# Wider source elements in the contiguous loads of a two-branch attention kernel

## The chip, the cores and the metric

The kernel runs on one core of a Trainium2 chip. The metric is the device time in microseconds (us). Runs of the kernel before spread by about 1%. Every comparison below was made on one chip in alternating rounds. Words used throughout: PE is the matrix engine, DVE the vector engine, ACT the scalar engine, POOL the general engine, and SP the engine whose instruction stream starts all loads here. The core has 16 DMA engines (the page gives the queues' share of 16). The tiles in the core's memory (SBUF) span 128 partitions here.

A load ("DMA") has a source access pattern and a destination access pattern. A *source element* here is one contiguous run of the source pattern, for example 8 KB. A *piece* is one contiguous run of the destination, inside one partition. The trace records *packets*, and we will see that a packet is one source element.

## The reference

Two attention branches share one output. Branch A has 32 query heads over 4 key/value heads, branch B has 32 of each. Both have 16 batches of 32 queries, 1024 cached keys and head size 128.

```python
q = (x @ wq).reshape(B, Sq, H, Dh).transpose(0, 2, 1, 3)
scores = einsum("bhqd,bhkd->bhqk", q, k_cache) * Dh ** -0.5
o = einsum("bhqk,bhkd->bhqd", softmax(scores), v_cache)
out = o.transpose(0, 2, 1, 3).reshape(B, Sq, H * Dh) @ wo
# result: concatenate([A's out, B's out], axis=-1); all bfloat16
```

B's K and V caches alone are 134 MB each, so of the 342 MB that the kernel moves almost four fifths are B's K and V.

## The kernel before

SP issues all loads in one order that a list scheduler fixed beforehand. A load waits on SP until its buffer is free, and everything behind it in SP's stream waits too: in the profile before SP waits 347 us in all, 101 us of it at B's K loads for DVE's transposes, which free K's buffers. B's K has two buffers of 1 MB, B's V three of 1 MB (four loads of 256 KB each), A's K two and A's V one of 256 KB.

```python
def folded_load(e, dst, src):                       # source and destination patterns given as they are
    inst = mybir.InstDMACopy(..., engine=mybir.EngineType.SP, queue="qSPDynamicHW",
        ins=e.lower_ap_dma(src), outs=e.lower_ap_dma(dst))
    return e.add_instruction(inst)
...
KB_sb = sb("KB_sb", [P, NKB, 2, 16 * Dh], BF)       # P = 128 partitions, 8 KB each per buffer
VB_sb = sb("VB_sb", [P, NVB, 4, NCH, Dh], BF)       # 2 KB per partition and head
...
# B's K: 128 source elements of 8 KB -> 128 partitions of 8 KB
ksrc = pb["k"][q.b, q.h0:q.h0 + 4].rearrange("a (p s) d -> (a p) (s d)", s=32)
... e.dma_start(KB_sb[:, sl, :, :].rearrange("p i n -> p (i n)"), ksrc)
# B's V, one head: 32 source elements of 8 KB -> 128 partitions of 2 KB
vsrc = pb["v"][q.b, q.h0 + t_].rearrange("(g p c) d -> g (p c d)", p=4, c=NCH)
... folded_load(e, VB_sb[:, sl, t_, :, :].rearrange("p c d -> p (c d)"), vsrc)
# A's K and V, output weights, x: 128 source elements of 2 KB -> 128 partitions of 2 KB
... e.dma_start(KA_sb[:, sl, :, :], pa["k"][q.b, q.s].rearrange("(p c) d -> p c d", c=NCH))
... e.dma_start(woB_sb[:, h_, :], wo[r0:r0 + Dh, :])
```

So V was already "folded": one source element covers four neighbouring partitions. The q weights (wq) have strided 2 KB rows and stay as they are.

## Time and profile before

| | before |
|---|---|
| time, median of 4 runs | 850.96 us |
| DMA rate over the span | 402 GB/s |
| PE, DVE, ACT busy | 85%, 64%, 53% |
| data packets of 2 KB / 8 KB | 34560 / 32768 |

First the page of the kernel before: the slices (40 equal parts of the span; a digit is the busy share in tenths), the DMA summary with the traffic of the chip's main memory (HBM), and the chain that ended last, followed back from the last instruction to whatever released each step.

```profile
PE   3999999799988799789988788987999867877777
...
DMA  9999999999999999999999999999999999999995
GB/s 346 384 389 404 410 397 398 414 403 391 411 414 417 417 409 415 414 382 403 419 414 415 412 417 418 409 411 417 419 420 415 407 417 419 408 390 410 418 413 195
DMA packets 82075, 341.59 MB, mean 402 GB/s; under 512 B 14112, under 2 KB 14624, under 8 KB 49184
...
HBM read 337.64 MB, written 2.10 MB: 400 GB/s over the span
...
DMA 48%; PE 28%; DVE 12%; SPq 6%; issue 3%; ACT 2%; POOL 0%; POOLq 0%; DVEq 0%
DMA KB_sb<-in_B_k_cache_dram 28%; DVE KBt_sb L844 9%; DMA VB_sb<-in_B_v_cache_dram 8%; PE ps_pj L674 7%; DMA woB_sb<-in_B_wo_dram 6%; PE ps_s L879 5%; DMA VA_sb<-in_A_v_cache_dram 4%; SPq L498 4%; PE ps_pj L731 4%; PE ps_o L971 3%; PE ps_kt L937 2%; PE ps_pt L921 2%; PE ps_s L862 2%; DMA KA_sb<-in_A_k_cache_dram 1%; DMA acc<-in_B_x_dram 1%
```

The DMA engines are busy all the time, at 400 to 420 GB/s in most slices, and nearly half of the chain is DMA, the largest part of it waiting for B's K. The kernel is bound by its loads, with PE not far behind.

Then the longest waits of consumers for B's loads (who waited for what; us in total, times, longest), and the issue of loads on SP (duration of the instruction in ns as min/median/max, then first and last start).

```profile
DVE KBt_sb L844 <- DMA KB_sb<-in_B_k_cache_dram: 62.6, 67, 3.3
...
PE ps_o L971 <- DMA VB_sb<-in_B_v_cache_dram: 29.5, 27, 3.3
```

```profile
L809 SPq DMA_DIRECT2D KB_sb<-in_B_k_cache_dram x128: 327/334/1511, 14.9 to 822.9; - x128
...
DMA to landing us min/median/max: 5.1/8.6/13.5
```

A load lands 8.6 us after its issue, so some 3.5 MB are on the way at any time (an estimate: 8.6 us at 402 GB/s).

The trace also records each packet's start, duration and size. The two numbers to take from these records are the duration and the *step*, which is the time from one packet's start to the next one's on the same engine. The records do not name the engine, so the step was read as the peak in the distribution of start differences.

| packet (before) | median duration, ns | mean duration, ns | step, ns |
|---|---|---|---|
| 2 KB | 84 | 85.5 | 80 |
| 8 KB | 309 | 317.3 | 306 |
| semaphore write (4 bytes) | 9 | 9.0 | 6 |

The counts fit only if a packet is a *source* element. V's 8 KB sources, which are written as four 2 KB pieces, show as 16384 packets of 8 KB.

### The profile page before, as it was taken

Reading aid. Unit: us, or ns where it says so; the run is one execution under the profiler, and the core shown is the slowest. Engines: PE = TensorE matmul, PEld = TensorE weight load, DVE = VectorE, ACT = ScalarE, POOL = GpSimd, SP = SyncE. Lnnn points to the kernel's source line nnn. Section 1 sums busy time; section 2 is a strip of 40 time slices with the busy share of each in tenths; the row PEclk is TensorE's granted clock in tenths of the full one; section 3 lists DMA queues with packets and bytes.
Section 4 is the critical chain, followed back from the end, with each engine's and each line's share of the span. In section 5 each row is a group of like instructions: output and inputs, shape, how many; then the busy total and the mean of one; then the engine's idle time right before and its main releaser. Section 6 shows DMA issues by size and latency. Waiting matters only on the chain.

```text
span 849.6 us, 27817 instructions
## 1 busy us (share of the span) xinstructions
PE 722.7 (85%) x12104; PEld 430.9 (51%) x12104; DVE 544.4 (64%) x1117; ACT 448.5 (53%) x981; POOL 68.2 (8%) x76
## 2 busy tenths in 40 slices
PE   3999999799988799789988788987999867877777
PEld 2556655456545455445654445553655544544443
DVE  0655676467755677457785566775677756757854
ACT  1455666366644466445655445754565635555453
POOL 0000000000000000000000000000000000000000
PEclk9999999999999999989999999999999989999999
DMA  9999999999999999999999999999999999999995
GB/s 346 384 389 404 410 397 398 414 403 391 411 414 417 417 409 415 414 382 403 419 414 415 412 417 418 409 411 417 419 420 415 407 417 419 408 390 410 418 413 195
DMA packets 82075, 341.59 MB, mean 402 GB/s; under 512 B 14112, under 2 KB 14624, under 8 KB 49184
## 3 DMA queue, kind: packets, MB, share of 16 engines
q1 hardware_dynamic: 81952, 339.80, 99.3%
q8 instruction: 96, 1.57, 0.7%
q14 instruction: 27, 0.22, 0.1%
HBM read 337.64 MB, written 2.10 MB: 400 GB/s over the span
## 4 chain that ended last, share of the span: by engine, by line
DMA 48%; PE 28%; DVE 12%; SPq 6%; issue 3%; ACT 2%; POOL 0%; POOLq 0%; DVEq 0%
DMA KB_sb<-in_B_k_cache_dram 28%; DVE KBt_sb L844 9%; DMA VB_sb<-in_B_v_cache_dram 8%; PE ps_pj L674 7%; DMA woB_sb<-in_B_wo_dram 6%; PE ps_s L879 5%; DMA VA_sb<-in_A_v_cache_dram 4%; SPq L498 4%; PE ps_pj L731 4%; PE ps_o L971 3%; PE ps_kt L937 2%; PE ps_pt L921 2%; PE ps_s L862 2%; DMA KA_sb<-in_A_k_cache_dram 1%; DMA acc<-in_B_x_dram 1%
## 5 line engine op out<-in xcount | busy, mean ns | idle before, releaser
L844 DVE STREAM_TRANSPOSE KBt_sb<-KB_sb 128x1024 f32<-128x1024 f32 x256 | 306.4, 1226 | 70.6 <-DMA KB_sb<-in_B_k_cache_dram 62.6
L902 ACT ACTIVATE P_sb<-ps_s 128x512 bf16<-128x512 f32 x256 | 151.8, 598 | 84.7 <-PE ps_s L879 73.7
L894 ACT ACTIVATE PTA_sb<-ps_s 128x1024 bf16<-128x1024 f32 x128 | 131.6, 1028 | 91.6 <-PE ps_s L862 73.7
L879 PE MATMUL ps_s<-KBt_sb,QB_sb 32*32 32x512 bf16 x4096 | 144.1, 388 | 9.4 <-DVE KBt_sb L844 4.6
L674 PE MATMUL ps_pj<-xT_sb,wq_sb 128*128 128x512 bf16 x448 | 121.0, 385 | 14.1 <-DMA wq_sb<-in_B_wq_dram 4.6
L818 POOL COPY VAp_sb<-VA_sb 128x1024 bf16<-128x1024 bf16 x64 | 66.7, 1042 | 762.3 <-DMA VA_sb<-in_A_v_cache_dram 735.8
L604 ACT COPY PT_sb<-ps_pt 128x512 f32<-128x512 f32 x128 | 75.0, 586 | 97.9 <-PE ps_o L971 80.6
L971 PE MATMUL ps_o<-VB_sb,PT_sb 128*32 128x128 bf16 x4096 | 82.3, 222 | 34.0 <-DMA VB_sb<-in_B_v_cache_dram 29.5
L921 PE MATMUL ps_pt<-id,P_sb 128*128 128x128 f32 x512 | 100.1, 302 | 8.5 <-ACT P_sb L902 5.7
L971 PEld LDWEIGHTS ps_o<-VB_sb,PT_sb 128*32 128x32 bf16 x4096 | 60.4, 97 | 71.4 <-issue 66.3
L921 PEld LDWEIGHTS ps_pt<-id,P_sb 128*128 128x128 f32 x512 | 79.4, 206 | 27.7 <-ACT P_sb L902 10.2
L862 PE MATMUL ps_s<-QT_sb,KTA_sb 128*128 128x256 bf16 x512 | 84.0, 275 | 7.3 <-ACT PTA_sb L894 5.1
L937 PE MATMUL ps_kt<-VAp_sb,PTA_sb 128*128 128x129 bf16 x1024 | 76.4, 221 | 7.9 <-ACT KTA_sb L604 2.6
L987 DVE TENSOR_SCALAR OB_sb<-ps_o,rinv_all 128x128 bf16<-128x128 f32 x128 | 44.0, 344 | 58.6 <-PE ps_o L971 57.2
L937 PEld LDWEIGHTS ps_kt<-VAp_sb,PTA_sb 128*128 128x128 bf16 x1024 | 64.4, 98 | 33.5 <-POOL VAp_sb L818 12.9
L879 PEld LDWEIGHTS ps_s<-KBt_sb,QB_sb 32*32 32x32 bf16 x4096 | 49.1, 89 | 62.2 <-issue 9.8
L731 PE MATMUL ps_pj<-woB_sb,OTB_sb 128*128 128x512 bf16 x240 | 68.2, 390 | 7.5 <-DMA woB_sb<-in_B_wo_dram 5.2
L674 PEld LDWEIGHTS ps_pj<-xT_sb,wq_sb 128*128 128x128 bf16 x448 | 40.3, 108 | 50.2 <-DMA wq_sb<-in_B_wq_dram 7.7
L742 DVE TENSOR_TENSOR acc<-acc,ps_pj 128x512 f32<-128x512 f32 x64 | 43.0, 672 | 30.4 <-PE ps_pj L731 30.2
L731 PE MATMUL ps_pj<-woA_sb,OTA_sb 128*128 128x512 bf16 x224 | 57.1, 379 | 3.7 <-DMA woA_sb<-in_A_wo_dram 1.9
L862 PEld LDWEIGHTS ps_s<-QT_sb,KTA_sb 128*128 128x128 bf16 x512 | 44.9, 98 | 29.0 <-ACT PTA_sb L894 9.1
L907 DVE TENSOR_TENSOR stat<-stat 64x1 f32<-64x1 f32 x256 | 41.9, 164 | 18.2 <-ACT P_sb L902 10.2
(52 smaller groups left out, 521.6 us busy)
## 6 DMA issues: line engine op xcount, KB each, us to landing
KB_sb<-in_B_k_cache_dram SPq DMA_DIRECT2D x128, 1024.0 KB, 8.6
VB_sb<-in_B_v_cache_dram SPq DMA_DIRECT2D x512, 256.0 KB, 8.5
KA_sb<-in_A_k_cache_dram SPq DMA_DIRECT2D x64, 256.0 KB, 9.2
VA_sb<-in_A_v_cache_dram SPq DMA_DIRECT2D x64, 256.0 KB, 8.8
wq_sb<-in_B_wq_dram SPq DMA_DIRECT2D x16, 512.0 KB, 10.3
woB_sb<-in_B_wo_dram SPq DMA_DIRECT2D x32, 256.0 KB, 9.8
woA_sb<-in_A_wo_dram SPq DMA_DIRECT2D x32, 256.0 KB, 8.7
wq_sb<-in_A_wq_dram SPq DMA_DIRECT2D x12, 512.0 KB, 10.0
```

What stands on the lines that cost most here:

```text
L604: pr.add("act", lambda e: e.copy(dst_ap, src_ap), reads=reads, writes=writes, name=name + "@act", wtag=wtag, rtag=rtag)
L674: last = e.matmul(ps_pj[:, 0:NTOK], pick(src, j), xT_sb[:, pi, j, :], start=(j == 0), stop=(j == DJ - 1))
L731: last = e.matmul(ps_a[:, 0:OUTW], OT[:, gp, hh, :], wo_[:, hh, oh * OUTW:(oh + 1) * OUTW], start=(hh == 0), stop=(hh == nh - 1))
L818: pr.add("pool", lambda g: g.tensor_copy(VAp_sb[:, sl, :, 0:Dh], VA_sb[:, :, :]), reads=["VA"], writes=[("VAp", sl)], name="VAp_cp", rtag= ...
L844: pr.add("dve", lambda e: e.transpose(KBt_sb[:, sl, t_, :].bitcast(F32).rearrange("p (s r i) -> p s r i", r=2, i=32), KB_sb[:, rs, t_, :]. ...
L862: last = e.matmul(ps_s[:, sbf, c2, i * 2 * P:(i + 1) * 2 * P], KTA_sb[:, sl, c * P:(c + 1) * P], qt, start=True, stop=True)
L879: last = e.matmul(ps_s[32 * cg:32 * cg + 32, sbf, g, :].rearrange("p (sh cl j) -> p sh cl j", sh=4, cl=4), lhsT, kt[32 * a:32 * a + 32, g, ...
L894: pr.add("act", lambda e: e.activation(dst, src, ACTF.Exp, scale=scale), writes=BK_S[sbf] + [("PTA", q.half)], name="expA", rtag={("Sv", s ...
L902: pr.add("act", lambda e, src=src, dst=dst, g=g: e.activation(dst, src, ACTF.Exp, scale=scale, accum_out=st[:, g:g + 1]), writes=[BK_S[sbf ...
L921: last = e.transpose(ps_pt32[:, m * P:(m + 1) * P], p32[:, m:Sk // 2:NPK], id32[:])
L937: last = e.matmul(ps_kt[:, qh * OA0:qh * OA0 + Dh + 1], PTA_sb[:, h, c, qh * P:(qh + 1) * P], VAp_sb[:, sl, 4 * h + c, 0:Dh + 1], start=(h ...
L971: last = e.matmul(ps_o[32 * a:32 * a + 32, 0:Dh], PT_pairs[:, c // 2, 32 * (a ^ (c // 4 * 2)):32 * (a ^ (c // 4 * 2)) + 32, c % 2], VB_sb[ ...
```

## The change

The intent: each packet has a fixed cost (4.7 ns, from the steps of 80 and 306 ns above), so use fewer and longer packets. V, A's K and V, the output weights and x get 16 source elements of 16 KB per 256 KB load, B's K gets 32 of 32 KB. The destination stays one run per partition, so 16 source elements cover eight neighbouring partitions each.

```diff
-def folded_load(e, dst, src):
+def wide_load(e, dst, src, groups=16):
     inst = mybir.InstDMACopy(
         ...
-        ins=e.lower_ap_dma(src), outs=e.lower_ap_dma(dst))
+        ins=e.lower_ap_dma(src.rearrange("(g n) d -> g (n d)", g=groups)), outs=e.lower_ap_dma(dst))
...
-    e.dma_start(woA_sb[:, h_, :], wo[r0:r0 + Dh, :])                      # woB, x, A's K and V likewise
+    wide_load(e, woA_sb[:, h_, :], wo[r0:r0 + Dh, :])
...
-    ksrc = pb["k"][q.b, q.h0:q.h0 + 4].rearrange("a (p s) d -> (a p) (s d)", s=32)
-    e.dma_start(KB_sb[:, sl, :, :].rearrange("p i n -> p (i n)"), ksrc)
+    ksrc = pb["k"][q.b, q.h0:q.h0 + 4].rearrange("a n d -> (a n) d")
+    wide_load(e, KB_sb[:, sl, :, :].rearrange("p i n -> p (i n)"), ksrc, 32)
...
-    vsrc = pb["v"][q.b, q.h0 + t_].rearrange("(g p c) d -> g (p c d)", p=4, c=NCH)
-    folded_load(e, VB_sb[:, sl, t_, :, :].rearrange("p c d -> p (c d)"), vsrc)
+    vsrc = pb["v"][q.b, q.h0 + t_]
+    wide_load(e, VB_sb[:, sl, t_, :, :].rearrange("p c d -> p (c d)"), vsrc)
```

More of the change, by code (lines that the diff above doesn't have):

```diff
@@ L611, in xT_stage @@
             for tc in range(NG):
-                pr.add("sp", lambda e, tc=tc: e.dma_start(xst[:, tc, :], xfs[pi][tc * P:(tc + 1) * P, :]),
+                pr.add("sp", lambda e, tc=tc: wide_load(e, xst[:, tc, :], xfs[pi][tc * P:(tc + 1) * P, :]),
                        writes=accres if tc == 0 else [("xst", pi, tc)], reads=[] if tc == 0 else accres, dma_key=f"x{pi}_{tc}", name="x_dma", dur=P * D * 2)
@@ L700, in th @@
                 def th(h_=h_, r0=r0):
-                    pr.add("sp", lambda e: e.dma_start(woA_sb[:, h_, :], wo[r0:r0 + Dh, :]),
+                    pr.add("sp", lambda e: wide_load(e, woA_sb[:, h_, :], wo[r0:r0 + Dh, :]),
                            writes=[("woA", h_)], dma_key=f"woA{h_}", name="woA_dma", dur=Dh * D * 2, wtag={("woA", h_): s_})
@@ L710, in th @@
                 def th(h_=h_, r0=r0):
-                    pr.add("sp", lambda e: e.dma_start(woB_sb[:, h_, :], wo[r0:r0 + Dh, :]),
+                    pr.add("sp", lambda e: wide_load(e, woB_sb[:, h_, :], wo[r0:r0 + Dh, :]),
                            writes=[("woB", h_)], dma_key=f"woB{h_}", name="woB_dma", dur=Dh * D * 2, wtag={("woB", h_): m_})
@@ L803, in st_dmaK @@
                 sl = q.kvslot
-                pr.add("sp", lambda e: e.dma_start(KA_sb[:, sl, :, :], pa["k"][q.b, q.s].rearrange("(p c) d -> p c d", c=NCH)),
+                pr.add("sp", lambda e: wide_load(e, KA_sb[:, sl, :, :].rearrange("p c d -> p (c d)"), pa["k"][q.b, q.s]),
                        writes=[("KA", sl)], dma_key=f"ka{sl}", name="ka_dma", dur=Sk * Dh * 2, wtag={("KA", sl): q.kid})
@@ L807, in st_dmaK @@
                 sl = q.krslot
-                ksrc = pb["k"][q.b, q.h0:q.h0 + 4].rearrange("a (p s) d -> (a p) (s d)", s=32)
-                pr.add("sp", lambda e: e.dma_start(KB_sb[:, sl, :, :].rearrange("p i n -> p (i n)"), ksrc), writes=[("KB", sl)], dma_key=f"kb{sl}", name="kb_dma", dur=4 * Sk * Dh * 2, wtag={("KB", sl): q.kid})
+                ksrc = pb["k"][q.b, q.h0:q.h0 + 4].rearrange("a n d -> (a n) d")
+                pr.add("sp", lambda e: wide_load(e, KB_sb[:, sl, :, :].rearrange("p i n -> p (i n)"), ksrc, 32), writes=[("KB", sl)], dma_key=f"kb{sl}", name="kb_dma", dur=4 * Sk * Dh * 2, wtag={("KB", sl): q.kid})
         def st_dmaV(q):
@@ L815, in st_dmaV @@
                 sl = q.kvslot
-                pr.add("sp", lambda e: e.dma_start(VA_sb[:, :, :], pa["v"][q.b, q.s].rearrange("(p c) d -> p c d", c=NCH)),
+                pr.add("sp", lambda e: wide_load(e, VA_sb[:, :, :].rearrange("p c d -> p (c d)"), pa["v"][q.b, q.s]),
                        writes=["VA"], dma_key="va", name="va_dma", dur=Sk * Dh * 2, wtag={"VA": q.kid})
@@ L822, in st_dmaV @@
                 for t_ in range(4):
-                    vsrc = pb["v"][q.b, q.h0 + t_].rearrange("(g p c) d -> g (p c d)", p=4, c=NCH)
-                    pr.add("sp", lambda e, t_=t_, vsrc=vsrc: folded_load(e, VB_sb[:, sl, t_, :, :].rearrange("p c d -> p (c d)"), vsrc), writes=[("VB", sl, t_)],
+                    vsrc = pb["v"][q.b, q.h0 + t_]
+                    pr.add("sp", lambda e, t_=t_, vsrc=vsrc: wide_load(e, VB_sb[:, sl, t_, :, :].rearrange("p c d -> p (c d)"), vsrc), writes=[("VB", sl, t_)],
                            dma_key=f"vb{sl}_{t_}", name="vb_dma", dur=Sk * Dh * 2, wtag={("VB", sl, t_): q.kid})
```

## The prediction

> **What bounds the kernel.** The DMA engines. In the forty slices their busy share reads 9 tenths in all but the last; the DMA summary gives 341.59 MB at a mean 402 GB/s, 410 to 420 in most slices. The chain of waits gives DMA 48%, PE 28%, DVE 12%. PE is busy 85% and DVE 64%; both have slack.
>
> **What a packet costs, from the trace's packet records.** A packet is one source element: the V loads, with 8 KB sources and 2 KB destinations, make 8 KB packets that are not slower than B's K packets (8 KB on both sides). On one engine the next packet starts 80 ns after a 2 KB packet, 306 ns after an 8 KB one, 6 ns after a semaphore write. A straight line through the first two is 4.7 ns per packet plus 37.7 ns per KB. [...]So only the constant can be saved: bytes, destination elements and semaphore writes stay.
>
> **What the change removes (source packets):** B's K 16384 to 4096; B's V 16384 to 8192; A's K and V, output weights and x 25600 to 3200. Together 42880 fewer. wq keeps its 2 KB rows (8192 packets). 42880 x 4.7 ns / 16 engines = 12.5 us (estimate). The records' durations (84 and 309 ns) suggest 9 ns, 24 us, but successive records overlap by 4 ns.
>
> **What it adds.** Issue time: loads whose source and destination counts differ (V) take a median 594 ns to issue, equal counts 327 (B's K) to 440 ns (A's, output weights). If all become about 600 ns, SP issues some 65 us more in all (estimate); it waits over 300 us for buffers, so most is hidden.
>
> **How much is on the critical path.** The packets at their cadence account for some 812 us of 849.6; the rest is the start (about 10 us), slow packets (mean 317 against 309 ns at 8 KB, about 17 us), and a short tail. Since the queue is nearly always full, nearly all of the 12.5 us should show, less perhaps 2 us given back where SP waits for DVE or PE (slices at 378 to 395 GB/s). 850 - 12.5 + 2 = 839 us, 1.2% faster.
>
> **What would show it right.** Data packets on the order of 43,000 fewer (about 39,000 in all); 16 KB packets with a cadence near 607 ns and 32 KB near 1210; plateau slices about 6 GB/s higher; V issues unchanged at about 0.6 us, B's K issues rising to it. DMA busy still 9 everywhere.
>
> **What would make it wrong.** (1) [...]packets stretch well over 607 ns and the kernel is over 2% slower. The trace does not show how partitions are dealt to engines; I keep a sixth for it. (2) [...](3) The per-packet saving may be the full 9 ns, or slow packets may become fewer: then 826 to 832 us, over 2% faster. (4) Compute may already bound more stretches than the 9s show: then nearly nothing is gained.
>
> Predicted: 839 us, 8 times in 10 within 829 to 862. Chances: faster by over 2% 0.14, within 2% 0.69, slower by over 2% 0.17.

The sum is 850 - 12.5 + 2 = 839.5, put down as 839 us.

## The result, and the profile after

The kernel after takes 1264.28 us (median of 4 runs, 1247.47 to 1277.11) against 850.96 us. The ratio is 1.478, with a 95% interval from 1.462 to 1.495. All ratios in this text are the mean time of one kernel's fast runs over that of the other's fast runs of the same rounds, so they are not quite the ratio of the medians quoted. The outputs are right.

The same lines of the page of the kernel after:

```profile
PE   4778775667665666575766655765676656666666
...
DMA  9999999999999899989999899899999999989996
GB/s 311 320 296 282 288 273 268 279 265 251 264 278 262 252 272 274 274 250 280 284 284 302 256 275 259 253 264 282 276 305 272 265 291 280 297 258 276 284 285 183
DMA packets 39195, 341.59 MB, mean 274 GB/s; under 512 B 14112, under 2 KB 14624, under 8 KB 23584
...
HBM read 337.64 MB, written 2.10 MB: 273 GB/s over the span
...
DMA 72%; DVE 9%; SPq 8%; PE 8%; issue 2%; ACT 0%; POOL 0%; POOLq 0%; DVEq 0%
DMA KB_sb<-in_B_k_cache_dram 45%; DMA VB_sb<-in_B_v_cache_dram 11%; SPq L499 8%; DVE KBt_sb L845 7%; DMA VA_sb<-in_A_v_cache_dram 5%; DMA KA_sb<-in_A_k_cache_dram 4%; DMA woB_sb<-in_B_wo_dram 3%; PE ps_pj L675 2%; DMA wq_sb<-in_B_wq_dram 2%; PE ps_s L880 1%; PE ps_pj L732 1%; DMA out_dram<-ost 1%; DMA acc<-in_B_x_dram 1%; PE ps_o L972 1%; PE ps_kt L938 1%
```

The packet count fell exactly as intended, by 42880. The bytes are the same and the engines still read as busy nearly everywhere, but they move 274 GB/s instead of 402. DMA is now 72% of the chain, 45% for B's K alone. The busy digits cannot tell the two kernels apart; the GB/s row does: nearly all 9s both times, but 400 against 273 GB/s of HBM traffic.

The waits for B's loads, and the issue of K's loads:

```profile
DVE KBt_sb L845 <- DMA KB_sb<-in_B_k_cache_dram: 286.9, 109, 6.5
...
PE ps_o L972 <- DMA VB_sb<-in_B_v_cache_dram: 154.4, 62, 5.7
```

```profile
L499 SPq DMA_DIRECT2D KB_sb<-in_B_k_cache_dram x128: 488/492/3572, 17.6 to 1213.2; - x128
...
DMA to landing us min/median/max: 8.5/14.2/23.6
```

DVE waits 287 us for K where it waited 63, PE waits 154 us for V where it waited 30, and a K load takes 14.2 us to land. The packet records say where that time is: packets of 2, 16 and 32 KB are stretched in the mean.

| packet (after) | undisturbed duration, ns | mean duration after, ns |
|---|---|---|
| 2 KB (wq and stores) | 84 | 106 |
| 16 KB | 611 (lowest hundredth of these packets in e5 below) | 951 |
| 32 KB | 1213 (lowest hundredth of these packets) | 1729 |

The wq packets were not changed by the diff at all, and they are stretched too. So the slowdown reaches loads that were not changed: something that the loads *share* got slower.

PE's granted clock also fell, from 0.986 to 0.842, while its busy share fell from 85% to 66%. That is not the cause of the loss, since PE is only 8% of the chain now.

### The profile page after: what moved, and what is told of

Same layout as the page of the kernel before. It is cut to its first block, busy times and chain, and to the rows that moved or that the text cites. A ratio compares the mean times of both kernels' runs of the same rounds, so it can differ in the third digit from the quotient of the medians.

```text
span 1245.7 us, 27694 instructions
## 1 busy us (share of the span) xinstructions
PE 827.0 (66%) x11981; PEld 479.6 (38%) x12104; DVE 551.2 (44%) x1117; ACT 453.4 (36%) x981; POOL 68.1 (5%) x76
## 2 busy tenths in 40 slices
DMA packets 39195, 341.59 MB, mean 274 GB/s; under 512 B 14112, under 2 KB 14624, under 8 KB 23584
## 4 chain that ended last, share of the span: by engine, by line
DMA 72%; DVE 9%; SPq 8%; PE 8%; issue 2%; ACT 0%; POOL 0%; POOLq 0%; DVEq 0%
DMA KB_sb<-in_B_k_cache_dram 45%; DMA VB_sb<-in_B_v_cache_dram 11%; SPq L499 8%; DVE KBt_sb L845 7%; DMA VA_sb<-in_A_v_cache_dram 5%; DMA KA_sb<-in_A_k_cache_dram 4%; DMA woB_sb<-in_B_wo_dram 3%; PE ps_pj L675 2%; DMA wq_sb<-in_B_wq_dram 2%; PE ps_s L880 1%; PE ps_pj L732 1%; DMA out_dram<-ost 1%; DMA acc<-in_B_x_dram 1%; PE ps_o L972 1%; PE ps_kt L938 1%
## 5 line engine op out<-in xcount | busy, mean ns | idle before, releaser
L972 PE MATMUL ps_o<-VB_sb,PT_sb 128*32 128x128 bf16 x4096 | 95.2, 244 | 157.0 <-DMA VB_sb<-in_B_v_cache_dram 154.4
L880 PE MATMUL ps_s<-KBt_sb,QB_sb 32*32 32x512 bf16 x4096 | 175.0, 460 | 23.0 <-DVE KBt_sb L845 14.1
L675 PE MATMUL ps_pj<-xT_sb,wq_sb 128*128 128x512 bf16 x408 | 130.2, 432 | 37.5 <-DMA wq_sb<-in_B_wq_dram 13.3
L972 PEld LDWEIGHTS ps_o<-VB_sb,PT_sb 128*32 128x32 bf16 x4096 | 71.5, 108 | 199.7 <-issue 195.0
L922 PE MATMUL ps_pt<-id,P_sb 128*128 128x128 f32 x512 | 111.0, 330 | 6.7 <-ACT P_sb L903 4.0
L938 PE MATMUL ps_kt<-VAp_sb,PTA_sb 128*128 128x129 bf16 x1024 | 87.7, 241 | 27.0 <-POOL VAp_sb L819 18.8
L938 PEld LDWEIGHTS ps_kt<-VAp_sb,PTA_sb 128*128 128x128 bf16 x1024 | 74.1, 109 | 59.6 <-POOL VAp_sb L819 35.7
L863 PE MATMUL ps_s<-QT_sb,KTA_sb 128*128 128x256 bf16 x512 | 91.8, 294 | 6.4 <-ACT PTA_sb L895 4.3
L836 PE MATMUL ps_kt<-ident,KA_sb 128*128 128x128 bf16 x512 | 48.2, 249 | 50.1 <-DMA KA_sb<-in_A_k_cache_dram 49.9
L605 ACT COPY OTB_sb<-ps_o 128x128 bf16<-128x128 bf16 x128 | 34.1, 266 | 88.9 <-PE ps_o L993 88.2
## 6 DMA issues: line engine op xcount, KB each, us to landing
KB_sb<-in_B_k_cache_dram SPq DMA_DIRECT2D x128, 1024.0 KB, 14.2
wq_sb<-in_B_wq_dram SPq DMA_DIRECT2D x16, 512.0 KB, 18.5
```

The source lines that it names most:

```text
L605: pr.add("act", lambda e: e.copy(dst_ap, src_ap), reads=reads, writes=writes, name=name + "@act", wtag=wtag, rtag=rtag)
L675: last = e.matmul(ps_pj[:, 0:NTOK], pick(src, j), xT_sb[:, pi, j, :], start=(j == 0), stop=(j == DJ - 1))
L863: last = e.matmul(ps_s[:, sbf, c2, i * 2 * P:(i + 1) * 2 * P], KTA_sb[:, sl, c * P:(c + 1) * P], qt, start=True, stop=True)
L880: last = e.matmul(ps_s[32 * cg:32 * cg + 32, sbf, g, :].rearrange("p (sh cl j) -> p sh cl j", sh=4, cl=4), lhsT, kt[32 * a:32 * a + 32, g, ...
L922: last = e.transpose(ps_pt32[:, m * P:(m + 1) * P], p32[:, m:Sk // 2:NPK], id32[:])
L938: last = e.matmul(ps_kt[:, qh * OA0:qh * OA0 + Dh + 1], PTA_sb[:, h, c, qh * P:(qh + 1) * P], VAp_sb[:, sl, 4 * h + c, 0:Dh + 1], start=(h ...
```

## The experiments

The theories (P, L and F stood at the start, Q came with e13):

- **P (partitions).** What costs is which partitions the elements of a load go to. By the patterns one of 16 outer source elements covers eight neighbouring partitions and one of 32 covers four. By P the packets of loads whose elements cover eight, or that go into 64 partitions at a time, are stretched, and so are packets in flight beside them.
- **L (length).** Long packets are slow in themselves.
- **F (fan-out).** A packet that is written as eight pieces is slow, one written as four is not.
- **Q (count).** 16 outer source elements are slow in themselves, whatever partitions they go to.

Fourteen kernels were run. Three of them (e4, e5, e6) put rows on other partitions than they should. The comparison with the reference still called them correct, so it is blind to the order of rows here. A likely reason: from the scales of the reference's random inputs the scores are about 0.001 (an estimate), so the softmax weights are nearly equal and the order hardly matters. All others except e9 to e11 pass as well, and their source and destination patterns list the same bytes in the same order as before.

### e1: B's K alone in 32 KB

```diff
-ksrc = ....rearrange("a (p s) d -> (a p) (s d)", s=32)
+ksrc = ....rearrange("a (p s) d -> (a p) (s d)", s=128)      # 32 source elements of 32 KB
```

> The kernel before with one part of the change: B's K from 32 source elements of 32 KB, everything else as before. Theory P[...]: no harm, 12288 packets fewer, 846 us +- 3, 32 KB packets of about 1210 ns. Rival L (long packets themselves are slow[...]): clearly slower, over 900 us, 32 KB packets well over 1300 ns in the mean. Rival F (slow when a source packet is written out as eight pieces rather than four): as P, since K makes four pieces.

Measured: 854.53 us against 851.22, ratio 1.004 (0.999 to 1.008). The 32 KB packets have a median of 1219 ns and a mean of 1256. The summary line of this run's page:

```profile
DMA packets 69787, 341.59 MB, mean 403 GB/s; under 512 B 14112, under 2 KB 14624, under 8 KB 49184
```

Even the longest packets run at full rate, so **L is out**. The small gain that I expected (846 us) did not come either; that is the second question below.

### e2: V alone in 16 KB

```diff
-vsrc = ....rearrange("(g p c) d -> g (p c d)", p=4, c=NCH)
+vsrc = ....rearrange("(g p c) d -> g (p c d)", p=8, c=NCH)   # 16 source elements of 16 KB
```

> The kernel before with V alone changed from 32 source elements of 8 KB to 16 of 16 KB. Theory P: V is 134 of 340 MB and the loads beside it are hit too[...], so most of a third to two thirds of the loss: 980 to 1150 us, 16 KB packets near 900 ns. Rival L: slow as well, 16 KB packets above 900 ns, but 8 KB packets of K stay at 309 ns. Rival F: as L.

Measured: 1225.93 us against 851.22, ratio 1.434 (1.424 to 1.443). So V alone brings nearly the whole loss, more than the 980 to 1150 us I expected. The profiled run was the slowest of its four (1233.71 us, called slow by the rule that a run over 1.5% above the fastest is). In it the 16 KB packets have a mean of 983 ns, and K's 8 KB packets, whose loads are those of before, 435 ns (before: 317).

```profile
DMA packets 73883, 341.59 MB, mean 277 GB/s; under 512 B 14112, under 2 KB 14624, under 8 KB 49184
```

K's packets were to stay at 309 ns under L. That they are stretched by V's loads again points to something shared.

### e3: 32 source elements everywhere

```diff
-def wide_load(e, dst, src, groups=16):
+def wide_load(e, dst, src, groups=32):        # on the kernel after
```

> The kernel after with 32 source elements in place of 16 everywhere (8 KB for V, A's K and V, output weights and x; B's K stays 32 KB). Theory P: fast and the best version, 31488 packets fewer than before, about 9 us saved: 841 us (836 to 847). Rival L: slow because of K's 32 KB, above 900 us. Rival F: as P, since every packet is written in four pieces.

Measured: 858.79 us against 851.22, ratio 1.009 (1.005 to 1.012). The one number 16 against 32 takes the kernel after from 1264 to 859 us.

```profile
DMA packets 50587, 341.59 MB, mean 397 GB/s; under 512 B 14112, under 2 KB 14624, under 8 KB 23584
...
DMA 49%; PE 23%; DVE 13%; SPq 8%; issue 3%; ACT 2%; POOL 1%; POOLq 0%; DVEq 0%
```

But it does not beat the kernel before, where I expected 841 us.

### e4: V as 16 outer elements of short packets

```diff
+VB_sb = sb("VB_sb", [P, NVB, 2, 4, NCH // 2 * Dh], BF)      # two 1 KB pieces per partition, apart
+vsrc = ....rearrange("(n g r) d -> g n (r d)", n=2, r=4 * NCH)   # 16 x 2 source elements of 8 KB
+... folded_load(e, VB_sb[:, sl, :, t_, :], vsrc)
```

> Wrong result on purpose (rows of V land on other partitions). V loads with 16 outer source elements of two 8 KB pieces each (strided), destination per partition two pieces of 1 KB. Packets stay 8 KB as before[...]. Theory P: slow like V in 16 KB, 980 to 1150 us, 8 KB packets of 400 to 500 ns in the mean. Rival L: packets are short, so as before, 845 to 860 us. Rival F: a packet is eight pieces (of 1 KB), so slow as well.

Measured: 1216.26 us, ratio 1.423 (1.414 to 1.432). Again this is slower than the 980 to 1150 us that I expected. The packets are 8 KB and as many as before, yet they take a mean of 450 ns (K's and V's together, which have one size; before: 317).

```profile
DMA packets 82075, 341.59 MB, mean 285 GB/s; under 512 B 14112, under 2 KB 14624, under 8 KB 49184
```

This is the mirror of e1: short packets, outer count 16, slow. Length and number of packets are both cleared. F is not, because each packet is eight pieces here.

### e5: B's K as eight pieces a packet, in 32 outer elements

```diff
+KB_sb = sb("KB_sb", [P, 4, NKB, 8 * Dh], BF)                # four 2 KB pieces per partition, apart
+ksrc = ....rearrange("(n a) (u r) d -> (a u) n (r d)", n=2, r=64)   # 32 x 2 source elements of 16 KB
 ...                                                         # each DVE transpose cut into two halves
```

> Wrong result on purpose (rows of K land on other partitions). The kernel before with B's K as 32 outer source elements of two 16 KB pieces, and a destination of four separate 2 KB pieces per partition: 16 KB packets that are written out as eight pieces of 2 KB each, as V's in the kernel after[...]. The DVE transposes are halved and doubled in number[...]. Theory P: the packets stay near 609 ns (mean under 660) and the time within 3% of before. Rival F (eight pieces a packet are slow): 16 KB packets of 900 ns and more, over 1000 us.

Measured: 867.57 us, ratio 1.018 (1.013 to 1.023). The 16 KB packets have a median of 626 ns and a mean of 653, with the same size and the same eight 2 KB pieces as V's in the kernel after (951 there).

```profile
DMA packets 73885, 341.61 MB, mean 395 GB/s; under 512 B 14112, under 2 KB 14624, under 8 KB 49184
```

**F is out** as far as the number of pieces goes. The eight pieces are not spread alike, though: if a copy pairs source and destination in flat order, as the failure of e9 below (relative error 0.63) suggests, they lie in two partitions here and in eight in the kernel after. By the same order a packet of e4 covers only four partitions, as before, and is slow (450 ns in the mean), so a packet need not cover eight to be stretched; e4's outer element, two packets, covers eight. The run also doubles DVE's transposes in number, so the 1.8% is not read as a cost of the packets.

### e6: the control for e4's strided form

```diff
-vsrc = ....rearrange("(n g r) d -> g n (r d)", n=2, r=4 * NCH)   # e4
+vsrc = ....rearrange("(n g r) d -> g n (r d)", n=2, r=2 * NCH)   # 32 x 2 source elements of 4 KB
```

> Wrong result on purpose. The control for the strided V of e4: the same strided destination of two 1 KB pieces per partition and a strided source, but 32 outer source elements of two 4 KB pieces. Theory P: not the pieces of 1 KB made e4 slow but its 16 outer elements; here within 2% of before (855 us, 16384 packets more at 4.7 ns are 5 us). If 1 KB pieces or the strided form are the cause (rival F in its weaker form): over 1000 us as e4.

Measured: 861.89 us, ratio 1.010 (1.004 to 1.015). The 4 KB packets take a mean of 165 ns.

```profile
DMA packets 98460, 341.59 MB, mean 397 GB/s; under 512 B 14113, under 2 KB 14625, under 8 KB 81953
```

So neither the 1 KB pieces nor the strided form made e4 slow. With eight pieces cleared by e5, its 16 outer elements are what is left. (Eight pieces of 1 KB in 32 elements were not run.)

### e7, e13, e14: half the partitions at a time

These runs test the other half of P, that a load into half the partitions is slow whatever the count of its elements. Each 1 MB load of B's K becomes two loads of 64 partitions.

```diff
+for hf in range(2):
+    folded_load(e, KB_sb[64 * hf:64 * hf + 64, sl, :, :]..., ksrc[n * hf:n * hf + n, :])
 # e7: n = 16 source elements of 32 KB;  e13: n = 32 of 16 KB;  e14: n = 64 of 8 KB (plain form)
```

> e1 with each 1 MB load of B's K cut into two loads of 64 partitions (0 to 63, 64 to 127), 16 source elements of 32 KB each; result correct. Packets (32 KB) and pieces (four of 8 KB) are those of e1[...]. Theory P[...]: [...]32 KB packets well above 1213 ns (1600 to 2400 in the mean), 950 to 1150 us. If [...]: 128 more issues of 0.5 us, at most 870 us.

(The condition is that P is wrong.)

> e7 with 32 source elements of 16 KB per load of 64 partitions in place of 16 of 32 KB; result correct. Theory P[...]: as slow as e7, 1150 to 1260 us, 16 KB packets of 900 to 1200 ns in the mean. Rival Q (16 outer elements as such are slow): 860 to 880 us with 16 KB packets near 615 ns.

> The kernel before with each load of B's K cut into two plain loads of 64 partitions, 64 source elements of 8 KB each, equal counts on both sides; result correct. Theory P: slow, 1100 to 1260 us, 8 KB packets well above 309 ns in the mean (K and V share that size: 400 to 480 ns). Rival Q: 850 to 870 us.

| | time of 4 runs, us | before, us | mean packet of K, ns | undisturbed, ns |
|---|---|---|---|---|
| e7, 16 x 32 KB | 1183.07 to 1244.12 | 851.18 | 2061 | 1213 |
| e13, 32 x 16 KB | 1364.04 to 1393.20 | 852.54 | 1186 | 611 |
| e14, 64 x 8 KB | 1365.80 to 1385.13 | 852.54 | 520 (K and V together) | 309 |

The runs of e7 and e13 differ among themselves by more than 1.5%, so these two got no ratio; e14's is 1.620 (1.610 to 1.629). The e13 profile is of a run called slow. The DMA summaries of e7, e13 and e14, and the issue of e14's K loads:

```profile
DMA packets 71836, 341.61 MB, mean 289 GB/s; under 512 B 16160, under 2 KB 16672, under 8 KB 51232
...
DMA packets 75931, 341.60 MB, mean 247 GB/s; under 512 B 16160, under 2 KB 16672, under 8 KB 51232
...
DMA packets 84124, 341.61 MB, mean 250 GB/s; under 512 B 16160, under 2 KB 16672, under 8 KB 51232
...
L498 SPq DMA_DIRECT2D KB_sb<-in_B_k_cache_dram x256: 465/596/2902, 13.8 to 1330.1; - x128
```

In size and number e14's data packets are those of the kernel before. The 2048 more under 512 B are semaphore writes, 16 for each of the 128 additional loads, as for every load before (14112 for 882 transfers).

All three are slow, and all three slower than the ranges that I gave. With plain patterns, 8 KB packets and 64 source elements, merely sending a load into 64 partitions at a time costs over 500 us. The 128 additional issues cannot explain it: e14's K loads have a median issue of 596 ns, so even all 256 are 153 us of SP's time, while the 8 KB packets themselves are stretched by two thirds. Nor can the smaller loads (in the kernel before V's loads are 256 KB, and it moves 402 GB/s), or where the data are read: e14 reads the same 8 KB source elements as the kernel before. **Q is out as an explanation of these runs**: the count of 16 is not needed for the stretch, the set of partitions is enough. And again loads that were not touched are stretched: V's 8 KB packets take a mean of 387 ns in e7 and 465 in e13, against 317 for 8 KB before, and the 2 KB packets (A's K and V, output weights, x, wq, stores) 98 and 113 ns against 86. K's packets alone do not explain the size of the loss: twice the step of 306 ns for each of K's 16384 packets (e13's take 1.9 times as long as undisturbed ones, 1186 against 611 ns) would add 313 us (an estimate) and give some 1164 us; e14 took 1376, so the other loads pay too.

### e12: the kernel after with V put back

```diff
-... wide_load(e, VB_sb[:, sl, t_, :, :]..., vsrc)
+... wide_load(e, VB_sb[:, sl, t_, :, :]..., vsrc, 32)
```

> The kernel after with V alone put back to 32 source elements of 8 KB; A's K and V, output weights and x keep 16 (about 52 of 340 MB). Theory P: [...]they are few and come singly: 890 to 1000 us, and the 8 KB packets of V[...] are stretched in part (mean 330 to 380 ns) while A's loads are in flight. If V alone were to blame (something special to V's tile): about 850 to 860 us.

Measured: 1019.88 us against 850.87, ratio 1.198 (1.192 to 1.203), above the expected 890 to 1000 us. The loads that keep 16 elements are 3200 packets of 16 KB, 52 of the 342 MB, and they cost 20%. V's 8 KB packets take 361 ns in the mean and K's 32 KB packets 1451, though both have the patterns of e3.

```profile
DMA packets 47387, 341.59 MB, mean 337 GB/s; under 512 B 14112, under 2 KB 14624, under 8 KB 23584
```

So V's tile is not needed for a loss. These loads too are stretched themselves (16 KB packets: 934 ns in the mean, 611 undisturbed), and so is what is in flight beside them.

### e8 to e11: where the small gain went

e1 and e3 removed 12288 and 31488 packets and were not faster. I summed each packet at its undisturbed step ("own time") and, apart from it, the part of each duration above the undisturbed one ("stretch"), per engine. SP's issue time is the sum over its DMA instructions. Each row but the ratio is of one profiled run: of the six runs of each experiment, e1's and e10's are the fastest and e3's (861.73 us) is the slowest, so a few us of stretch can be chance.

| | packets' own time, us | stretch, us | SP's issue time, us | ratio to before |
|---|---|---|---|---|
| before | 812.8 | 21.5 | 503 | 1 |
| e1, K folded | 809.3 | 23.7 | 530 | 1.004 |
| e3, all by 32 | 803.8 | 34.7 | 553 | 1.009 |
| e8, SP delayed | 813.0 | 26.6 | 475 + the added increments | 1.005 |
| e9, V in pairs | 811.1 | 18.5 | 360 | 0.993 |
| e10, e3 + V in pairs | 802.1 | 24.2 | 399 | 0.996 |
| e11, e1 + V in pairs | 807.6 | 22.1 | 382 | 0.994 |

By this account e3 saved 9 us of own time, and 13 us of stretch took it back. The issue of a load with unequal counts on the two sides is longer: K's median went from 334 to 472 ns.

```profile
L499 SPq DMA_DIRECT2D KB_sb<-in_B_k_cache_dram x128: 471/472/1260, 15.6 to 832.9; - x128
```

Theory S says that SP, which issues in order, now feeds the queue later, so that engines run dry for moments and the next packets are slow, as they are at the start. In the kernel before, 73 of the 746 packets of 2 KB in the first 5 us of loading took over 120 ns, up to 575, instead of 84. And somewhat more of the stretch lies where few loads are outstanding (issued and not landed; the mean is nine): with fewer than nine outstanding the kernel before spends 43% of its time and 12.8 us of its stretch, e3 48% of its time and 23.0 us.

e8 delays SP in the kernel before:

```diff
+def slow_start(e, dst, src):
+    for _ in range(3):
+        e.sem_inc(IDLE[0], 1)
+    return e.dma_start(dst, src)          # for B's K, A's K and V, output weights, x
```

> About the missing gain of e3, not the large loss. The kernel before with three semaphore increments on SP ahead of each load of B's K, A's K and V, output weights and x (328 loads), which makes these loads issue later, as the unequal counts did in e1 and e3 (SP issue time 503 us before, 530 in e1, 553 in e3). Theory S (SP's in-order issue time feeds the DMA queue late, so engines run dry): slower than before by 0.5 to 2%, and more stretched packets where few loads are outstanding. If issue time is harmless: same as before within 0.3%.

Measured: 856.76 us against 851.18, ratio 1.005 (1.001 to 1.010), stretch 26.6 us. The direction is that of S, but the test is weak: the load instructions themselves became shorter behind the increments (475 us in all against 503), so the delay was smaller than planned.

e9 to e11 go the other way and join two heads' V loads into one, which halves V's issues (a median 607 ns for two heads in e9, 594 for one before):

```diff
+for t_ in (0, 2):
+    vsrc = pb["v"][q.b, q.h0 + t_:q.h0 + t_ + 2].rearrange("h (g r) d -> g h (r d)", r=4 * NCH)
+    folded_load(e, VB_sb[:, sl, t_:t_ + 2, :, :].rearrange("p t c d -> p t (c d)"), vsrc)
```

> The kernel before with the V loads of two heads joined into one load: 32 outer source elements of two pieces of 8 KB (one per head), destination two pieces of 2 KB per partition. 256 loads in place of 512; packets and bytes as before, 4096 semaphore writes fewer. Theory S (SP's issue time feeds the DMA queue late): SP's issue time falls from 503 to about 380 us, fewer stretched packets, 840 to 850 us. If issue time is harmless, or the coarser loads cost as much: same as before within 0.3%.

> e3 (32 source elements everywhere) with V in pairs of heads as in e9. Theory S: the packet saving of e3 (the packets' own time fell by 9 us from before to e3) is no longer eaten by late issues: 836 to 846 us, faster than before and than e3. Rival R (long or folded packets are themselves stretched now and then, whatever SP does): no faster than e9, about 850 to 860 us.

> e1 (only B's K folded, 32 KB) with V in pairs of heads. Theory S: between e9 and e10, 840 to 848 us. Rival R: at or above e9.

These three give a wrong result (relative error 0.63): most likely the copy pairs source and destination in flat order, so the two heads' rows are mixed. They are of use for timing only. e9 takes 844.69 us against 849.46, ratio 0.993 (0.989 to 0.997); e10 847.03, ratio 0.996 (0.991 to 1.001); e11 845.63, ratio 0.994 (0.989 to 0.998). SP's share of the chain falls with its issue time, from 6% before and 8% in e3 to 3% in e10:

```profile
DMA 49%; PE 31%; DVE 14%; SPq 3%; ACT 2%; issue 2%; POOL 0%; DVEq 0%; POOLq 0%
```

With V in pairs, folding everything by 32 costs 0.3% (e10 against e9, as ratios of medians) instead of 0.9% (e3 against before). The direction is that of S, and e9 is faster than before as S expected. But the two costs differ by less than their intervals, and pairing V also halves its number of loads and of semaphore writes, so S is supported and not shown. It is not the whole story either: e10 was not faster than e9, although its packets' own time is 9 us less and only three of its six runs fell into the expected 836 to 846 us. What the rest of the stretch is stays open.

No correct version that was run beats the kernel before; the best is e1, which is the same within noise. Whether V in pairs, done correctly, keeps the 0.7% of e9 was not tried.

## Why the prediction was wrong

The prediction was 839 us, 829 to 862, with 0.17 for "slower by over 2%". It was 1264 us.

- **What bounds the kernel** was right, and so was **what a packet is**: 82075 - 39195 = 42880 fewer, as counted beforehand.
- **The fixed cost of 4.7 ns a packet** fits the steps of undisturbed packets: their lowest clear peaks are at 607 ns for 16 KB (e5) and 1209 for 32 KB (e1), within 2 ns of the line through 2 and 8 KB (the highest peaks are a little later, at 622 and 1215). The 9.0 us of e3 is a sum of such steps, so it is no second test, and no run became faster by it.
- **The failed step** is the sentence "So only the constant can be saved: bytes, destination elements and semaphore writes stay", together with "nearly all of the 12.5 us should show". It took the 37.7 ns per KB as a property of the bytes. It is a property of the bytes *and of the partitions that a load's elements go to*. The change kept the destination runs, but a 16 KB packet with 2 KB for each partition covers eight of them by the patterns, and the time per KB rose: 951 ns instead of 611 for 16 KB, 1729 instead of 1213 for 32 KB.
- **Point (1) of "what would make it wrong" named what happened**: packets well over 607 ns (951 measured) and a kernel over 2% slower (ratio 1.478). It got a sixth of the chance and none of the range.
- **Issue time** was predicted at about 600 ns for all; K's rose to 492 ns in the kernel after, and 472 in e3. (Its 327 ns for B's K is the minimum; the median is 334.) "Most is hidden" may have been too kind: longer issue is the candidate for what took back the packet saving of e1 and e3, but this is not shown.
- **Instruction fetches** (point 2, cut): the trace has packets of 16 KB in an instruction queue (96 in the page), which took a mean of 976 ns before and 1214 after, so they are stretched too. What that cost was not tested.
- **Full 9 ns per packet, compute already binding** (points 3 and 4): neither was tested by itself, and neither is needed for the loss; e1 and e3 have PE busy 85% as before.

What is shown: that 16 outer elements are the harmful part (e2, e3, e4), that packet length, packet count and fan-out are not (e1, e4, e5, e6), that loads are slowed which were not changed (wq in the kernel after, K in e2, V in e7), and that sending a load into half the partitions also does large damage, with 16, 32 or 64 elements (e7, e13, e14). What is not shown: why the partitions matter, since no record names the engine or the partition of a packet. Even which partitions an element covers is read from the patterns; the comparison with the reference is no witness, since it passed e4 to e6. Nor did any run give a load of 128 partitions 16 outer elements that cover other than eight neighbouring partitions each, so for such loads Q is out only by analogy with e13 and e14. P gives the direction of every large loss seen here, and no run contradicts it. It doesn't give the sizes: all six slow experiments (e2, e4, e7, e12, e13, e14) were slower than the range I had set down.

## What to carry to other kernels

When loads fill the DMA engines, look at how many partitions an outer source element covers, and how many the load goes to, before lengthening source elements: in this kernel 32 outer elements per 128 partitions (four neighbouring partitions each) kept the rate with packets up to 32 KB (403 GB/s in e1, 397 in e3, 402 before), while 16 (eight each) lost a third of it (274 GB/s), with unchanged loads slowed too. Judge DMA by GB/s and by the duration of a packet of known size, not by busy digits: they read 9 nearly everywhere at 402 and at 274 GB/s. And a saving of a few ns per packet is easily lost: e3's packets should have saved 9 us and it was 0.9% slower, with K's issue 138 ns longer (472 against 334 ns) as one possible reason.
